# Polysketch attention and a gated FFN in one kernel: batch 0's W from Gram matrices, PSUM copies for VectorE, later key batches in single pieces

## The chip, the cores and the metric

The kernel runs on one core of a Trainium2 chip. The metric is device microseconds of one execution. Kernels are compared on one chip with their runs side by side. Names: TensorE (PE; PEld is its weight load), VectorE (DVE), ScalarE (ACT), GpSimd (POOL), SyncE (SP). SBUF is the working memory, PSUM the memory that matmuls write.

## The reference, cut to what matters

Inputs: q, k, v of 4 batches, 4 heads, 1088 positions, 32 columns; S1, S2 of 8 x 32; three FFN weights (128 x 1536, 128 x 1536, 1536 x 128). All are fp32.

```
phi(x)[.., (i, j)] = a[.., i] * b[.., j]     with a = S1 x, b = S2 x     (r = 8, so 64 features)
kv  = sum over s of phi(k)[s, f] * v[s, d]
z   = sum over s of phi(k)[s, f]
num = phi(q) kv;  den = phi(q) z + 1e-6;  attn = num / den
x   = attn, heads side by side: 4352 rows of 128
out = (relu(x @ w_gate) * (x @ w_val)) @ w_out
```

z as an 8 x 8 matrix Z[i, j] is the sum of a_i b_j over the positions, that is S1 (sum of k k^T) S2^T. The denominator needs no features: phi(q) z = sum over j of b_j(q) (W q)_j, with W[j, d] = sum over i of Z[i, j] S1[i, d]. The kernel calls the 32 x 8 block W of a head "w" and puts it beside S1 and S2 in the stationary operand `wst`, so that one query sketch gives a, b and W q.

## The kernel before, in words

All is laid out by a planner. `Plan.add(engine, cost, function, deps, due, take, give, at)` collects steps, and `Plan.run` (L33) orders them with those costs by the earliest start, among steps within 0.6 us of it by the latest start that `due` allows. Costs, due times (`T0 + PACE * i` for block i of the FFN, L252, L602) and landing times (`land`) only set the order of instructions on each engine; on the chip semaphores hold each instruction until its inputs are there. Where the plan leaves TensorE idle before the first queries are done, matmuls on a zero tile (`warm`, L215, L650) are put in its stream.

PSUM: two double banks `dbl` (slots "V": values, sketches), two single banks `sgl` (slots "G": half a gate each), `o_ps` for the output and `m_ps` (slot "M", one only: sums over keys, transposes of query features, numerators). A step that takes a slot keeps it until a later step gives it back.

Loads: S1 and S2 to `s16`; batch 0's keys in four loads (`load_k`, L138, one for each head) and one for the last 64 rows (`load_kr`), on SP, ScalarE and POOL; the first 8 of 34 query columns of batch 0 (L168), `v32` in two loads. Gate and value weights come on POOL in 8 + 4 blocks of 128 columns, `wo` between. The rest of q, k is issued on SP in order, the rest of v on POOL.

One key batch, class `K` (L255): `t1` transposes 32 x 32 blocks on VectorE, so that head and column lie on the partitions; `sketch` (TensorE, fp32) forms a and b for two pairs of heads; `t2` transposes them back to positions on the partitions (`abk`). `zsum` (L357) sums a b^T over the positions in `m_ps`, `zevac` masks it to heads on VectorE, `w` (L372) multiplies by S1, `wevac` copies it to `wst` on ScalarE. `phi` (L351) forms the features a_i b_j by a broadcast product (`outer`, L245) on POOL, one piece of batch 0 on VectorE; `kv` (L383) sums features times v in `m_ps`; `kvevac` (L392) masks and scales them to `kv_bd` on VectorE. The batch is cut in two pieces (`cuts`). `m_ps` is held from `zsum` to `kvevac`.

The queries go in nine groups, class `Q` (L414): one of 8 columns (256 rows), then eight of 16 (512 rows). `t1`, `sketch` (with `wst`), `t2`, then `bwm`, `red`, `rec`, `am` for 1/den times a, `phi`, `tr` (transposes of the features on TensorE, L503), `tre` (copy on ScalarE), `num`, and `x`, the copy that makes the FFN's input `xT`.

The FFN runs in 51 blocks: `gate` (two halves of 512 columns in two G slots, L553), `relu` on ScalarE, `val` (a V slot), `prod` on VectorE (L565), `outp` (eight matmuls, L570), and at a group's end `oevac` and `store`.

## Time and profile before

| | |
|---|---|
| median of 3 runs | 118.71 us (118.59 to 119.12) |
| the profiled execution | 119.1 us |
| its span | 117.3 us, 3396 instructions |
| DVE busy | 90.3 us, of it products of the FFN (L567) 61.6 |
| ACT busy | 75.6 us, of it relu (L563) 56.2 |
| POOL busy | 51.9 us, of it features of keys 17.8, of queries 17.2 |
| matmuls on zeros (L217) | 190, 14.4 us |
| moved by DMA | 9.49 MB, nearly all before 33 us |

How to read it: times are from the start of the span. Matmuls overlap in the pipeline, so that a row's length for TensorE is longer than the step to the next row; a run of matmuls is read by the distance of its starts. fp32 matmuls are two instructions each. "L" is a line of the kernel. "idle before <- X" names what ended an engine's idle time.

### The profile page before, as it was taken

How to read it: one execution, taken by the hardware profiler on the slowest of the kernel's cores; microseconds unless marked ns; L12 is line 12 of the kernel's file. 1: busy time of each engine (PE TensorE's matmuls, PEld its weight loads, DVE VectorE, ACT ScalarE, POOL GpSimd, SP SyncE). 2: the span in 40 equal slices, each digit the busy share in tenths (PEclk: the TensorE clock that was granted, in tenths of full speed). 3: DMA queues.
4: the chain of work that ended last, by engine and by line, in shares of the span. 5: the costliest groups of instructions: out<-in, count | busy, mean ns of one | idle time of the engine just before them, and what ended most of it. 6: DMA issues, size and time to landing. Idle time of an engine off the chain costs nothing. (4 is left out here: it accounts for less than half of the span.)

```text
span 117.3 us, 3396 instructions
## 1 busy us (share of the span) xinstructions
PE 109.1 (93%) x1381; PEld 72.2 (62%) x1381; DVE 90.3 (77%) x145; ACT 75.6 (64%) x137; POOL 51.9 (44%) x73
## 2 busy tenths in 40 slices
PE   6989999999999999999899999998999999999930
PEld 6968889776665556566555556674566555655620
DVE  4067498687999899669988986799699589678830
ACT  0413003867857996548779874587797897988720
POOL 5708999796360178813401886153107018000000
PEclk9999999999999999999999999999999999999995
DMA  2999999999930030002000300030002003003003
GB/s 75 225 285 261 221 205 219 258 201 228 219 72 0 0 89 8 0 6 67 22 0 6 92 0 6 0 89 0 6 21 69 3 0 92 3 0 95 0 0 89
DMA packets 10908, 9.49 MB, mean 81 GB/s; under 512 B 4420, under 2 KB 9156, under 8 KB 10892
## 3 DMA queue, kind: packets, MB, share of 16 engines
q1 hardware_dynamic: 5364, 6.30, 21.6%
q0 software_dynamic: 4576, 2.05, 13.6%
q10 hardware_dynamic: 952, 0.92, 3.1%
q8 instruction: 10, 0.16, 0.6%
q14 instruction: 6, 0.05, 0.2%
HBM read 9.05 MB, written 2.23 MB: 96 GB/s over the span
## 5 line engine op out<-in xcount | busy, mean ns | idle before, releaser
L567 DVE TENSOR_TENSOR ht<-g_sb,d_ps 128x1024 f16<-128x1024 f16 x51 | 61.6, 1215 | 13.8 <-ACT g_sb L563 9.6
L563 ACT ACTIVATE g_sb<-g_ps 128x512 f16<-128x512 f32 x102 | 56.2, 597 | 16.2 <-PE g_ps L550 15.0
L576 PEld LDWEIGHTS <-ht 128*128 128x128 f16 x408 | 26.7, 113 | 11.3 <-DVE ht L567 3.0
L550 PE MATMUL g_ps<-xT,wg 128*128 128x512 f16 (+1 forms) x108 | 33.2, 368 | 0.2
L576 PE MATMUL o_ps<-wo,ht 128*128 128x128 f16 x408 | 31.2, 220 | 0.8 <-DVE ht L567 0.7
L550 PE MATMUL d_ps<-xT,wv 128*128 128x512 f16 (+1 forms) x108 | 30.3, 367 | 0.0
L246 POOL TENSOR_TENSOR kp<-abk 128x640 f16<-128x640 f32 (+1 forms) x15 | 17.8, 1213 | 5.5 <-DVE abk L347 5.5
L246 POOL TENSOR_TENSOR qp<-an,abq 128x512 f16<-128x512 f32 (+1 forms) x17 | 17.2, 1032 | 0.6
L217 PE MATMUL o_ps<-zero 128*128 128x128 f16 x190 | 14.4, 240 | 1.1 <-DVE mask L201 1.1
L550 PEld LDWEIGHTS <-wv 128*128 128x128 f16 x108 | 9.9, 99 | 7.9 <-issue 1.7
L482 POOL TENSOR_TENSOR bw<-abq 128x128 f32<-128x128 f32 x8 | 3.7, 457 | 24.8 <-DVE abq L472 24.8
L510 ACT COPY pt<-m_ps 128x1024 f16<-128x1024 f16 (+1 forms) x9 | 8.7, 965 | 8.3 <-PE m_ps L506 8.2
L217 PEld LDWEIGHTS <-zero 128*128 128x128 f16 x190 | 12.8, 109 | 2.0 <-DVE mask L201 1.1
L550 PEld LDWEIGHTS <-wg 128*128 128x128 f16 x108 | 8.7, 98 | 5.0 <-issue 1.8
L494 POOL TENSOR_TENSOR an<-abq,rd 128x128 f32<-128x128 f32 x8 | 3.3, 408 | 15.1 <-DVE rd L490 9.6
L472 DVE STREAM_TRANSPOSE abq<-d_ps 128x512 f32<-128x512 f32 (+1 forms) x9 | 6.1, 680 | 1.6 <-PE d_ps L465 1.6
L582 ACT ACTIVATE o_sb<-o_ps 128x512 f32<-128x512 f32 (+1 forms) x9 | 5.1, 572 | 2.1 <-PE o_ps L576 2.0
L506 PE MATMUL m_ps<-ident,qp 128*128 128x128 f16 x68 | 5.3, 219 | 0.9 <-DVE kv_bd L393 0.9
L456 DVE STREAM_TRANSPOSE qT<-qA 128x512 f32<-128x512 f32 (+1 forms) x9 | 5.9, 659 | 0.2 <-DMA qA<-in_q_dram 0.2
L465 PE MATMUL d_ps<-qT,wst 64*64 64x256 f32 (+7 forms) x96 | 5.8, 334 | 0.2 <-ACT wst L379 0.2
L506 PEld LDWEIGHTS <-qp 128*128 128x128 f16 x68 | 4.3, 97 | 2.4 <-issue 1.7
L525 ACT CAST xT<-m_ps 128x512 f16<-128x512 f32 (+1 forms) x9 | 5.2, 578 | 0.6 <-PE m_ps L518 0.6
(67 smaller groups left out, 69.9 us busy)
## 6 DMA issues: line engine op xcount, KB each, us to landing
kA<-in_k_dram SPq DMA_DIRECT2D x14, 128.0 KB, 4.5
out_dram<-o_sb SPq DMA_DIRECT2D x28, 64.0 KB, 1.7
qA<-in_q_dram SPq DMA_DIRECT2D x12, 136.0 KB, 7.2
v_sb<-in_v_dram POOLq DMA_DIRECT2D x3, 256.0 KB, 13.5
v<-in_v_dram ACTq DMA_DIRECT2D x1, 512.0 KB, 7.4
qA<-in_q_dram SPq DMA_DIRECT2D x4, 104.0 KB, 5.3
wo<-in_moe_w_out_dram POOLq DMA_DIRECT2D x1, 384.0 KB, 7.3
kA<-in_k_dram ACTq DMA_DIRECT2D x2, 128.0 KB, 5.3
```

Source lines behind the costliest of these rows:

```text
L217: nc.tensor.matmul(o_ps[:, 0], zero, zero, start=True, stop=True)
L246: eng.tensor_tensor(out=dst.rearrange("p x (i j) -> p x i j", i=R), in0=a[:, :, :, None].to_broadcast([128, n, R, R]), in1=b[:, :, None, : ...
L456: nc.vector.transpose(self.qT.rearrange("p n t -> p (n t)"), qA[:, self.n0:self.n0 + self.nn].rearrange("p n d -> p (n d)"))
L465: nc.tensor.matmul(d[64 * c:64 * c + 64, hp, 32 * lo:32 * hi], wst[r, b].rearrange("p a f -> p (a f)"), self.qT[r].rearrange("p (n c) t -> ...
L472: nc.vector.transpose(self.ab.rearrange("p n a f -> p a n f"), ps(f"q{self.g}")[:, :, 0:32 * self.m].rearrange("p a (n t) -> p a n t", t=32))
L506: nc.tensor.transpose(t[:, 128 * i:128 * i + 128], self.qp[:, i].rearrange("p a f -> p (a f)"), ident)
L510: nc.scalar.copy(out=self.pt.rearrange("f n s -> f (n s)"), in_=m_ps.bitcast(FP16)[:, 0:128 * self.m])
L525: nc.scalar.copy(out=xT[:, 32 * self.n0:32 * (self.n0 + self.nn)].rearrange("p (a t s) -> p a t s", a=4, s=ns), in_=m_ps[:, 0:32 * self.nn ...
L550: nc.tensor.matmul(d[:, (y - lo) * W:(y - lo + 1) * W], w[:, js[y]], xT[:, xs], start=True, stop=True)
L563: nc.scalar.activation(out=g_t[i][:, z], in_=ps1(f"g{i}{z}"), func=ACTF.Relu)
L567: nc.vector.tensor_tensor(out=h_t[i].rearrange("p (a c) -> p a c", a=2), in0=g_t.pop(i), in1=ps(f"v{i}"), op=ALU.mult)
L576: nc.tensor.matmul(o_ps[:, s], ht[:, y * W + s:(y + 1) * W:ns], wo[:, j], start=(j == 0 and s == 0), stop=j == NJ - 1, skip_group_check=True)
```

## The change

The keys of batch 0 are loaded with positions on the partitions, as v is (`k_tok`), in one load of 512 KB on SP and one small one on ScalarE; the small first query load becomes four. A class `K0` takes batch 0. For the three later batches the two pieces become one, `zsum` writes four tiles of 32 rows in a G slot in place of two of 64 rows in `m_ps`, `w` is one matmul in place of two, and `kv_bd` is written by ScalarE in two halves. Where VectorE forms features (batch 0 and the first query group), ScalarE first copies b to a G slot, and VectorE reads it there.

Loads and set-up:

```diff
+    load_v(nc.sync, k_tok, 0, k)
     nc.scalar.dma_start(out=s16[0:R], in_=S1[:, None, :].to_broadcast([R, 4, D]))
-    nc.sync.dma_start(out=s16[R:2 * R], in_=S2[:, None, :].to_broadcast([R, 4, D]))
-    load_kr(nc.gpsimd, 0)
+    nc.scalar.dma_start(out=s16[R:2 * R], in_=S2[:, None, :].to_broadcast([R, 4, D]))
+    load_vr(nc.scalar, k_tok, 0, k)
     for h in range(H):
-        load_k((nc.sync, nc.scalar)[h % 2], 0, h)
-    nc.sync.dma_start(out=qA[:, 0:8, :],
...
+        load_q(nc.sync, 0, h, 0, 8)
     load_v(nc.scalar, v32, 0)
     load_vr(nc.sync, v32, 0)
...
-    warm(48)
+    warm(12)
     nc.tensor.transpose(st_ps, s16x, id32)
+    p_ps = sgl[1][:, 0:128]
+    nc.tensor.matmul(p_ps, s16x[0:R], s16x[0:R], start=True, stop=True)
...
+    st = sb("st", [128, 2 * R])
+    nc.scalar.copy(out=st, in_=st_ps)
+    for hf in range(2):
+        nc.vector.tensor_tensor(out=sk[:, hf, :, hf, :],
...
+    Pbd = sb("Pbd", [128, H, D])
+    nc.vector.tensor_tensor(out=Pbd, in0=p_ps.rearrange("p (h d) -> p h d", h=H),
+                            in1=mask4[:, :, None].to_broadcast([128, H, D]), op=ALU.mult)
...
+    warm(24)
...
-    T0 = 11.5
-    PACE = 1.5
+    T0 = 13.0
+    PACE = 1.4
```

The class for batch 0 (its plan, then the steps on the chip):

```diff
+            ta = add("DVE", 0.66, lambda: self.t1(0, 4), at=land)
+            gram = add("PE", 1.1, self.gram, take=("G", n + "g"), at=land + 0.1, lat=0.2)
...
+            gb = add("DVE", 0.3, self.gevac, [gram])
+            w1 = add("PE", 0.25, self.w1, [gb], lat=0.2)
+            e1 = add("ACT", 0.2, self.w1evac, [w1])
+            w2 = add("PE", 0.25, self.w2, [e1], lat=0.2)
+            self.wst = add("DVE", 0.2, self.wevac, [w2], give=(n + "g",))
+            cast = add("ACT", 1.15, lambda: nc.scalar.copy(out=v_sb[0], in_=v32), at=lvland)
...
+            ca = add("ACT", 0.22, lambda: self.bcopy(0), [ta2], take=("G", n + "b"), lat=0.2)
+            cb = add("ACT", 0.22, lambda: self.bcopy(1), [tb2], take=("G", n + "b"), lat=0.2)
+            pa = add("POOL", 1.06, lambda: self.phi(0, 1, "POOL"), [ta2])
+            pb = add("POOL", 1.06, lambda: self.phi(1, 1, "POOL"), [tb2])
+            da = add("DVE", 0.7, lambda: self.phi(0, 0, "DVE"), [ca])
+            db = add("DVE", 0.7, lambda: self.phi(1, 0, "DVE"), [cb], give=(n + "b",))
+            pr = add("POOL", 0.6, lambda: self.phi(2, 0, "POOL"), [tb2])
+            va = add("PE", 0.25, lambda: self.kv(0), [pa, da, cast], take=("M", n + "m"), lat=0.2)
+            vb = add("PE", 0.3, lambda: self.kv(1), [pb, db, pr, va], lat=0.2)
...
+        def gram(self):
+            d = ps1("k0g")
+            for c in range(NQ):
+                for h in range(H):
+                    nc.tensor.matmul(d[32 * h:32 * h + 32, 0:D], k_tok[:, h, c], k_tok[:, h, c],
+                                     start=c == 0, stop=c == NQ - 1)
...
+        def w1(self):
+            nc.tensor.matmul(ps1("k0g")[:, 64:64 + R], self.gbd.rearrange("p h d -> p (h d)"),
+                             st[:, R:2 * R], start=True, stop=True)
...
+        def w2(self):
+            nc.tensor.matmul(ps1("k0g")[:, 96:96 + R], Pbd.rearrange("p h d -> p (h d)"), self.m1,
+                             start=True, stop=True)
...
+        def sketch(self, x, hf):
+            nc.tensor.matmul(ps("k0")[:, x, 0:256], sk[:, hf].rearrange("p a b f -> p (a b f)"),
+                             self.kT[:, 4 * x + hf:4 * x + 4:2].rearrange("p c h t -> p c (h t)"),
+                             start=hf == 0, stop=hf == 1)
...
+        def bcopy(self, x):
+            nc.scalar.copy(
+                out=ps1("k0b")[:, 64 * x:64 * x + 64].rearrange("p (x j) -> p x j", j=R),
+                in_=self.ab[:, 2 * x:2 * x + 2, :, 0, R:2 * R].rearrange("p c h j -> p (c h) j"))
```

Here P is S1^T S1 (`Pbd`), so that W = P times Gram times S2^T, head by head. The later batches:

```diff
-        def __init__(self, b, land, cuts, engs):
+        def __init__(self, b, land, cuts):
...
+            ab = P.add("PE", 0.75, self.sketch, t1, take=("V", n), lat=0.2)
+            t2 = P.add("DVE", 0.8, self.t2, [ab], give=(n,))
+            z = P.add("PE", 0.65, self.zsum, [t2], take=("G", n + "z"), lat=0.2)
+            zm = P.add("DVE", 0.2, self.zevac, [z])
+            w = P.add("PE", 0.3, self.w, [zm], lat=0.2)
+            self.wst = P.add("ACT", 0.25, self.wevac, [w], give=(n + "z",))
...
+            kv = [P.add("PE", 0.6, self.kv, ph, take=("M", n + "m"), lat=0.2)]
+            kvx = P.add("ACT", 0.25, lambda: kvevac(b, 0), kv)
+            self.kvx = P.add("ACT", 0.25, lambda: kvevac(b, 1), [kvx], give=(n + "m",))
...
+        def zsum(self):
+            d = ps1(f"k{self.b}z")
+            for x in range(NQ):
+                for hp in range(2):
+                    a = self.ab[:, x, hp]
+                    r = 64 * (x % 2) + 32 * hp
+                    nc.tensor.matmul(
+                        d[r:r + 32, 0:2 * R].rearrange("f (h j) -> f h j", h=2),
+                        a.rearrange("p h f -> p (h f)"), a[:, :, R:2 * R],
+                        start=x < 2, stop=x > NQ - 3, skip_group_check=True)
...
+    def kvevac(b, g):
+        nc.scalar.mul(out=kv_bd[b][:, :, D * g:D * g + D],
+                      in_=m_ps[:, 0:128].rearrange("f (h g d) -> f h g d", h=2, g=2)[:, :, g],
+                      mul=maskkv[:, g, 0:1])
```

And the first query group's product on VectorE, with the landing times and the clocks at which the plan begins:

```diff
             if g == 0:
-                ph = [P.add("DVE", 0.62, lambda: self.phi(0, 3, "DVE"), [d4]),
+                bc = P.add("ACT", 0.22, self.bcopy, [t2], take=("G", n + "b"), lat=0.2)
+                ph = [P.add("DVE", 0.52, lambda: self.phi(0, 3, "DVE"), [d4, bc], give=(n + "b",)),
...
-    kk = [K(0, [5.4, 5.4, 5.4, 5.4, 8.5, 5.4], [0, 4, 9], [("DVE", "POOL"), ("POOL", "POOL")])]
-    qland = [7.0, 16.0, 20.0, 24.0]
+    kk = [K0(4.9, 8.0)]
+    qland = [6.5, 16.0, 20.0, 24.0]
...
-        kk.append(K(b, [[0, 14.0, 18.0, 22.0][b]] * 2, [0, 5, 9], [("POOL", "POOL")] * 2))
+        kk.append(K(b, [[0, 14.0, 18.0, 22.0][b]] * 2, [0, 5, 9]))
...
-    order = P.run({"PE": 5.3, "DVE": 5.2, "ACT": 5.2, "POOL": 5.2, "SP": 4.5})
-    pe = 5.3
+    order = P.run({"PE": 4.9, "DVE": 4.8, "ACT": 5.0, "POOL": 5.2, "SP": 4.5})
+    pe = 4.9
```

In the changed program TensorE's stream from the keys of batch 0 to the first gate reads: Gram, half of the sketch, the first W matmul, the other half, the second W matmul, the rest of the sketch, 9 fillers, first query sketch, `kv` first half, 33 fillers, `kv` second half, 19 fillers, second query sketch, transposes of the first queries, 17 fillers, numerator, 14 fillers, gate. On VectorE the transpose of the second query group's columns stands ahead of the first group's product, and on ScalarE the cast of v stands between the two copies of b.

## The prediction

> **What bounds the kernel now.** I read the page, then the timeline of the first 24 us, the chain of waits, and the tables of waits. In the page, the busy line and the chain's first line:
>
> ```profile
> PE 109.1 (93%) x1381; PEld 72.2 (62%) x1381; DVE 90.3 (77%) x145; ACT 75.6 (64%) x137; POOL 51.9 (44%) x73
> ...
> PE 27%; DVE 4%; ACT 3%; issue 1%; ACTq 0%
> ```
>
> TensorE is the engine with the least left (93%), and of the chain that ended last 27% of the span is TensorE against 4% VectorE and 3% ScalarE. That chain reaches back only to 72 us; what lies before is read from the timeline. Its columns are start, length, engine, line, and, last, the instructions merged.
>
> ```profile
> 1.06 4.93 PE L217 MATMUL o_ps<-zero 128*128 128x128 f16 x48 [1.06 <-DVE mask L201]
> ...
> 6.40 1.07 PE L217 MATMUL o_ps<-zero 128*128 128x128 f16 x16
> ...
> 7.25 1.31 DVE L316 STREAM_TRANSPOSE kT<-kA 128x512 f32<-128x512 f32 x2 [0.38 <-DMA kA<-in_k_dram]
> ...
> 9.74 1.15 ACT L304 CAST v_sb<-v 128x1152 f16<-128x1152 f32 x1 [3.03 <-DMA v<-in_v_dram]
> ...
> 10.37 2.98 POOL L246 TENSOR_TENSOR kp<-abk 128x640 f16<-128x640 f32 x2 [0.19 <-DVE abk L347]
> 10.54 1.66 DVE L246 TENSOR_TENSOR kp<-abk 128x512 f16<-128x512 f32 x1
> ...
> 12.47 0.71 DVE L456 STREAM_TRANSPOSE qT<-qA 128x512 f32<-128x512 f32 x1 [0.17 <-DMA qA<-in_q_dram]
> ...
> 13.14 0.57 PE L374 MATMUL m_ps<-zm,S1bd 128*128 128x16 f32 x4
> ...
> 14.23 0.45 PE L465 MATMUL d_ps<-qT,wst 64*64 64x128 f32 x8 [0.16 <-ACT wst L379]
> ...
> 17.62 0.39 PE L506 MATMUL m_ps<-ident,qp 128*128 128x128 f16 x4
> ...
> 19.91 0.60 PE L550 MATMUL g_ps<-xT,wg 128*128 128x256 f16 x4
> ```
>
> This shows two stages. Up to 19.91 us TensorE runs mostly matmuls on zeros (L217), and the first gate matmul (L550) waits for a chain: keys landed and transposed (7.25), products (10.37 and 10.54), W (13.14), the first query sketch (14.23), the transposes of the first query features (17.62). From there 2.3 us lead to the first gate. From 19.91 to 113.2 us TensorE is close to gapless: 51 blocks of gate, value and output matmuls cost 0.43 + 0.43 + 0.45 = 1.31 us each in the chain, 67 of 93 us, and key and query work fills most of the rest. The chain shows what else there is where a key batch ends:
>
> ```profile
> 77.69 0.23 PE g_ps L550
> 77.92 0.02 issue
> 77.95 0.61 ACT g_sb L563
> 78.55 0.02 issue
> 78.58 1.22 DVE ht L567
> 79.80 0.21 DVE kv_bd L393
> 80.01 0.04 issue
> 80.05 0.61 PE m_ps L506 x8
> ```
>
> TensorE's transposes (L506, at 80.05) wait for kv_bd (L393), which stands on VectorE behind a product of 1.22 us (L567). The table of waits prices that at 0.9 us over three batches:
>
> ```profile
> PE m_ps L506 <- DVE kv_bd L393: 0.9, 3, 0.3
> ```
>
> Last, SP's own queue in the first 20 us: a load stands still until v, 512 KB, has landed. The program's loads on SP and ScalarE take eight semaphores in turn, and each waits for the last user of its own.
>
> ```profile
> SPq L139 <- DMA v<-in_v_dram: 1.8, 1, 1.8
> ```
>
> So the time is the start (19.9 us) plus TensorE's work (93.3) plus the tail (4.1). The tail is the same in both orders.
>
> **The change, part by part. The start.** (1) *Keys of batch 0.* Now four loads of 128 KB on two queues; the second on ScalarE's queue lands 5.3 us after its issue at 1.85, so VectorE starts at 7.25, while SP's second (1.65) landed after 3.3, at 5.0. New: all 512 KB first on SP's queue, v behind only S and the 64 last rows on ScalarE's. Bounds: 5.0 (as SP's half now) and 7.2 (as now); I take 5.9, nearer the queue it is moved to. SP's four small q loads come behind, POOL loses one issue of 0.86.
> (2) *Set-up.* Twelve more memsets on VectorE: eight at 0.35/4, two at 0.06, one of 128x256 (0.27), one of 64x128 (0.17): 1.3 us, so they end at 4.5 instead of 3.2; then five masked products instead of two, 0.2 to 0.3 each, to about 5.7. Hidden by the wait for keys, with almost no margin: keys at 5.0 would cost 0.7. S is no limit: its two loads of 4 KB fit in what was moved between 1.0 and 2.3 us (17 GB/s, 22 KB); the second is now issued 0.6 later, so its transposes run near 3.2, with 24 fillers behind.
> (3) *Gram.* 36 fp32 matmuls; the trace shows two instructions per fp32 matmul (L374: x4 for two), so 72. Bounds: 16 instructions of L327 with 64x96 took 0.40 with 0.255 for one, 10 ns each; L361's 18 took 0.77 with 0.22 for one, 32 ns each. 0.7 to 2.3 us; I take 1.4. Sketch of batch 0: eight instructions of L465 with 64x256 took 0.66 on four tiles, so about 0.23 for a pass of 256 columns; two matmuls of full height are four passes, 0.9, twice, and 0.25 for the rest. With the two small W matmuls (0.2 each) TensorE needs 3.9 us from the keys on.
> (4) *W.* Five small steps replace t2, z and W: masked Gram, matmul, copy, matmul, masked copy. W is ready near 9.7 instead of 14.2, since it no longer waits for VectorE's product and for the 38 zero matmuls ahead of L374.
> (5) *b in PSUM.* VectorE's product of 512 took 1.66 beside POOL's (2.98 for two); the one of 384 (16.25, POOL only issuing a DMA) took 0.56, so 512 alone would be about 0.69. New: four of 256 at about 0.42, and two ScalarE copies (0.2 by L379). No less VectorE time, but POOL is not held: 4 x 0.65 + 2 x 0.44 = 3.5 for 4.05. The second copy stands behind the cast of v on ScalarE (1.15), so v's landing enters this path: 9.74 now, with 256 KB of keys ahead. New: 8.0 (those 256 KB at the 279 GB/s of 5 to 10 us, and half the queue's share) to 10.0 (issued 0.3 later); I take 9.0. Then cast to 10.15, copy, product to 11.2. POOL ends near 12.9, with the issue of wo (1.08) now between its products; so kv_bd stands near 14.
> (6) *The queue.* In SP's new order the third of the four wide q loads (columns 8 to 33) reuses v's semaphore, and the fourth and the keys of batch 1 stand behind it. Now only the second key load of batch 1 waits so (the 1.8 above). So they are issued at 9.05 to 9.9 and land 3.9 to 5.3 us later (shortest and median of the q loads): 14.4 against 12.47 now. That transpose (0.71) stands on VectorE ahead of the first queries' product, and the second query sketch on TensorE ahead of the transposes: 14.4 + 0.7 + 0.65 = 15.75 for the transposes, against 17.62.
> (7) From the transposes to the first gate nothing changes: 2.3 us. First gate at 18.1. TensorE's own string from the keys ends sooner: 3.9, 92 fillers at 0.055 (the row at 6.40: 1.07 less 0.24 for one, over 15), and 2.7 for two query sketches, kv, transposes and numerator make 11.7, so 17.6. Gain 1.8; bounds: 3.0 (keys at 5.0, v at 8.0) and 0 (v at 10.0, 5.3 more).
> (8) *POOL's queue.* The last third of wv is issued at 14.93 now, lands 8.2 later at 23.1, and is read at 23.5. New: issued near 14, read at 21.7; with the same 8.2 that is 0.5 late. But wo ahead of it is issued near 10.1 instead of 13.29, so I take 0 and keep 0.5 for the range.
>
> One row speaks against this part. The first 48 zero matmuls took 0.10 each (4.93 less 0.24, over 47), those at 6.40 0.055, though the page's clock row reads 9 in all these slices. The new kernel has 12, a gap, then 24. If half pace lasted through Gram and the first sketch, that is 1.4 + 0.9 = 2.3 more on TensorE's string, of which the wait for q hides 0.5: the gain would be 0. I take no loss, since fillers run from 1.0 on, and keep it as a rival. The Trainium skill (TensorE: Matmul & The Clock Gate, Part 1) has the clock halved until TensorE was busy through a window of about 3.4 us; counted from the gap's end near 3.2 that is an estimated 6.6, half of Gram at half pace, and a gain of 1.6 where the row alone lets me say 1.8.
>
> **The steady part,** three later batches. The W matmul is one, not two: two instructions fewer, 0.113 each (L374: 0.60 for four, 0.26 for one): -0.7. z: 36 instructions of 32-wide tiles for 18 of 64: at 10 to 32 ns, 0.36 to 1.15 for 0.58 a batch; I take 0.02 each, between the tile's own width and its full height, 0.7: +0.4 (-0.6 to +1.7). The Trainium skill (TensorEngine Tiling, Instruction Overhead) gives a matmul about 60 cycles however few its columns, and warns against tiling a dimension already small; at that page's rule, some 25 ns, z alone would be +1.0. Sketch and transposed copy in one piece: one start-up of 0.2 less a batch, -0.3 (0 to -0.6). kv_bd goes to ScalarE in two pieces (0.2 each for 0.28), behind a relu (0.60) instead of a product (1.22): of the 0.9 I take -0.4 (0 to -0.9). m_ps is no longer held from z to kv_bd (25.45 to 33.87 for batch 1), so query transposes can go earlier: -0.3 (0 to -1.0). z now holds one of the two gate buffers: a half gate must wait for a relu of 0.60; the order puts outputs of 0.45 between, so 0.1 a batch: +0.3 (0 to +1.5). New pacing constants only reorder work. Sum -1.0 (-3.8 to +2.5).
>
> **Sum.** The profiled execution took 119.1, span 117.3, so 1.8 lies around it; its span would go to 117.3 - 1.8 - 1.0 = 114.5, that is 116.3. The median of the runs is 118.71, 0.4 lower; taken off that: 115.9.
>
> **The rivals.** *The queue eats the start:* v lands no earlier and the wide q loads land at 15.5 or later; the first gate stays near 19.6. For: the 1.8 wait above and the slow landings; against: v has 256 KB less ahead. 118.7 - 0.3 - 1.0 = 117.4. *Half pace:* no gain at the start, 118.7 - 1.0 = 117.7. For: the 0.10 row; against: it must last 2.3 us past the keys, and TensorE has worked since 1.0 but for the gap. *Slower:* z in the gate buffer. From its matmuls to the copy of W, 2.3 us now (70.71 to 73.0), only one gate buffer is left; if each of four half gates then leaves TensorE idle for 0.38 (relu 0.60 less its own matmul 0.22), a batch loses 1.5, three 4.5, against 1.8 at the start and 1.3 of the steady part without this term: 118.7 - 3.1 + 4.5 = 120.1. It decides from 1.0 us a batch. For: half gates wait so in the chain now; against: outputs stand between. *It does not do what it says:* W was not what the first gate waited for: kv_bd is done at 17.0 now, the first queries' product at 17.3, and if these come no sooner the start gains nothing; with the steady part at the middle of its bounds (-0.6), 118.1.
>
> **How the numbers follow.** Forecast 0.63 (own range 114.0 to 117.3: the start between 1.0 and 2.7, the steady part within 1 of its value), queue 0.13, half pace 0.10, slower 0.08, nothing 0.06. Predicted 115.9. The range takes in the two rivals that eat the start and, below, half of the steady part's better bound: 113.8 to 118.0. A measurement tells 0.5%, 0.6 us, from no change: below 118.1 lie the forecast and most of the first two rivals, 0.83; within, 0.07; above 119.3 the slow rival and the upper tail of the forecast, 0.10.
>
> **What would show it.** The key transpose starting near 5.9; W's masked copy near 9.7; the first gate near 18.1, with the second query transpose waiting for q's DMA just before; the wait of the transposes for kv_bd gone from VectorE; z's 36 instructions near 0.9 us; no relu waits of TensorE around z. Wrong if the first gate stays past 19.5, or if the stretch from first gate to last output is not shorter than 93.3.

## The result: 0.6% faster, and where the gain went

Side by side on one chip, the kernel before took 119.16 us (median of 20 runs) and the changed one 118.56 us; the ratio is 0.9941, 95% interval 0.9915 to 0.9968. The forecast was 115.9 with a range of 113.8 to 118.0: the sign was right, the size was not. Ratios count only undisturbed runs, those within 1.5% of the fastest of their kernel; where that leaves out a whole group of a kernel's runs, its single times are given too.

The page of the changed kernel, busy line and the chain of work that ended last:

```profile
PE 105.0 (90%) x1337; PEld 71.1 (61%) x1337; DVE 90.6 (78%) x157; ACT 78.3 (67%) x149; POOL 50.6 (43%) x76
...
PE 54%; DMA 13%; DVE 11%; ACT 10%; SPq 4%; issue 3%; ACTq 1%; DVEq 0%
```

TensorE is busy for 4 us less than before, which is what the 62 fewer matmuls on zeros make up (14.4 us of busy time before, 10.2 now). But the chain, which reached back only to 72 us before, now goes back to the first load, with 13% of the span in transfers and 4% in SP's queue. So this chain can be read for the start; its columns are start, length and what:

```profile
1.46 0.30 ACTq L166
...
2.52 8.40 DMA v<-in_v_dram
...
10.93 0.31 SPq L154
...
12.44 0.54 SPq L140
...
15.14 0.42 SPq L154
...
16.54 6.79 DMA qA<-in_q_dram
...
23.45 0.06 DVE qT L560
...
24.09 1.18 DVE ht L678
...
27.32 0.55 PE o_ps L687 x8
```

v lands at 10.92. SP's third wide q load (L154) stands until then, behind it the keys of batch 1 (first issued at 12.44; before at 7.43), behind these batch 1's queries (15.14; before 11.75). The last of those lands at 23.3, and VectorE, which meets its transpose (qT) first, starts the FFN's product (ht) only at 24.09. TensorE's and VectorE's waits for it, with SP's own:

```profile
PE m_ps L232 <- DMA s<-in_S_dram: 2.8, 1, 2.8
PE d_ps L661 <- DVE ht L678: 1.1, 1, 1.1
...
DVE qT L560 <- DMA qA<-in_q_dram: 1.7, 1, 1.7
...
SPq L154 <- DMA v<-in_v_dram: 4.0, 1, 4.0
```

Beside that chain runs a second one, on TensorE, which sets the first gate. The timeline, in the columns of the first section (PE and one line of DVE):

```profile
5.37 0.25 PE L232 MATMUL m_ps<-id,s 16*128 16x16 f32 x1 [2.84 <-DMA s<-in_S_dram]
...
6.60 2.74 PE L227 MATMUL o_ps<-zero 128*128 128x128 f16 x24
9.27 1.19 PE L331 MATMUL g_ps<-k_tok 128*32 128x32 f32 x72
10.39 1.60 PE L357 MATMUL d_ps<-kT,sk 128*128 128x256 f32 x4
...
19.04 0.40 PE L617 MATMUL m_ps<-ident,qp 128*128 128x128 f16 x4
...
21.33 0.60 PE L661 MATMUL g_ps<-xT,wg 128*128 128x256 f16 x4
```

S's second load, issued at 1.46 behind the 512 KB of keys, lands at 5.3. TensorE stands for 2.84 us, then runs 24 zero matmuls at 0.107 us each, and Gram starts at 9.27. ("Half pace" is this distance of 0.107 us between the starts of two zero matmuls, "full pace" is 0.056; "the clock rose" names the moment at which one became the other.) The transposes of the first query features (L617) come at 19.04, before at 17.62.

| from the trace | before | changed |
|---|---|---|
| first gate matmul | 19.91 | 21.33 |
| last matmul of the first output block starts | 24.8 | 27.6 |
| last output matmul starts | 112.98 | 112.63 |
| from the second row to the third | 88.14 | 84.98 |

The expectations below call the second row "the eighth output block"; it is the eighth output matmul, the last of the first block. The start lost 2.8 us, the rest gained 3.16, and the span fell by 0.4 (117.3 to 116.9). The two parts are taken in turn.

### The profile page after: what moved, and what is told of

It reads as the page before. It is cut to its first block, busy times and chain, and to the rows that moved or that the text cites. A ratio compares the mean times of both kernels' runs of the same rounds, so it can differ in the third digit from the quotient of the medians.

```text
span 116.9 us, 3336 instructions
## 1 busy us (share of the span) xinstructions
PE 105.0 (90%) x1337; PEld 71.1 (61%) x1337; DVE 90.6 (78%) x157; ACT 78.3 (67%) x149; POOL 50.6 (43%) x76
## 4 chain that ended last, share of the span: by engine, by line
PE 54%; DMA 13%; DVE 11%; ACT 10%; SPq 4%; issue 3%; ACTq 1%; DVEq 0%
PE g_ps L661 16%; PE o_ps L687 15%; PE d_ps L661 13%; DVE ht L678 8%; ACT g_sb L674 8%; DMA v<-in_v_dram 7%; DMA qA<-in_q_dram 6%; PE d_ps L569 4%; SPq L154 2%; PE m_ps L617 2%; PE m_ps L629 2%; SPq L140 2%; PE m_ps L495 1%; ACT xT L636 1%; PE d_ps L441 1%
## 5 line engine op out<-in xcount | busy, mean ns | idle before, releaser
L674 ACT ACTIVATE g_sb<-g_ps 128x512 f16<-128x512 f32 x102 | 57.7, 601 | 14.2 <-PE g_ps L661 12.4
L661 PE MATMUL g_ps<-xT,wg 128*128 128x512 f16 (+1 forms) x108 | 35.4, 367 | 1.4 <-ACT g_sb L674 0.5
L687 PEld LDWEIGHTS <-ht 128*128 128x128 f16 x408 | 28.0, 112 | 10.9 <-DVE ht L678 1.0
L687 PE MATMUL o_ps<-wo,ht 128*128 128x128 f16 x408 | 31.0, 219 | 0.9 <-DVE ht L678 0.9
L586 POOL TENSOR_TENSOR bw<-abq 128x128 f32<-128x128 f32 x8 | 3.6, 456 | 27.6 <-DVE abq L576 27.5
L268 POOL TENSOR_TENSOR kp<-abk 128x640 f16<-128x640 f32 (+1 forms) x12 | 13.8, 1176 | 2.8 <-DVE abk L458 2.8
L661 PEld LDWEIGHTS <-wg 128*128 128x128 f16 x108 | 10.0, 100 | 5.6 <-issue 2.6
L227 PE MATMUL o_ps<-zero 128*128 128x128 f16 x128 | 10.2, 245 | 1.1 <-DVE mask L207 1.1
L227 PEld LDWEIGHTS <-zero 128*128 128x128 f16 x128 | 9.0, 112 | 1.4 <-DVE mask L207 1.1
L268 POOL TENSOR_TENSOR kp<-ab 128x256 f16<-128x256 f32 (+1 forms) x6 | 3.1, 551 | 8.1 <-DVE ab L367 8.1
L617 PE MATMUL m_ps<-ident,qp 128*128 128x128 f16 x68 | 5.5, 220 | 0.1
## 6 DMA issues: line engine op xcount, KB each, us to landing
v_sb<-in_v_dram POOLq DMA_DIRECT2D x3, 256.0 KB, 10.2
```

The source lines that it names most:

```text
L227: nc.tensor.matmul(o_ps[:, 0], zero, zero, start=True, stop=True)
L268: eng.tensor_tensor(out=dst.rearrange("p x (i j) -> p x i j", i=R), in0=a[:, :, :, None].to_broadcast([128, n, R, R]), in1=b[:, :, None, : ...
L617: nc.tensor.transpose(t[:, 128 * i:128 * i + 128], self.qp[:, i].rearrange("p a f -> p (a f)"), ident)
L661: nc.tensor.matmul(d[:, (y - lo) * W:(y - lo + 1) * W], w[:, js[y]], xT[:, xs], start=True, stop=True)
L674: nc.scalar.activation(out=g_t[i][:, z], in_=ps1(f"g{i}{z}"), func=ACTF.Relu)
L687: nc.tensor.matmul(o_ps[:, s], ht[:, y * W + s:(y + 1) * W:ns], wo[:, j], start=(j == 0 and s == 0), stop=j == NJ - 1, skip_group_check=True)
```

## Experiments on the start

All are compared with the kernel before; "first block" is the start of the last matmul of the first output block in the profiled execution. The stretch from there to the last output matmul was 84.98 or 84.99 in every run of this section but e13_warm40, where it was 85.85.

| run | change against the changed kernel | median us | ratio, 95% | first gate | first block |
|---|---|---|---|---|---|
| (changed) | | 118.56 | 0.994 (0.992-0.997) | 21.33 | 27.6 |
| e1_sfirst | S ahead of the keys | 115.72 | 0.968 (0.962-0.975) | 18.78 | 23.9 |
| e2_q | batch 0's q in two loads | 117.44 | 0.986 (0.982-0.990) | 20.61 | 26.2 |
| e3_sq | both | 114.91 | 0.963 (0.959-0.968) | 18.29 | 23.5 |
| e10_nofill | 24 zero matmuls taken out | 118.40 | 0.991 (0.986-0.995) | 21.95 | 27.5 |
| e13_warm40 | zero matmuls 40 + 0 for 12 + 24 | 120.39 | 1.000 (0.993-1.007) | 19.75 | 28.4 |
| e17_qwarm | two q loads, 48 + 0 | 118.37 | 0.988 (0.981-0.996) | 21.75 | 26.9 |
| e19_s2sp | S2 on SP's queue behind the keys | 118.74 | 0.992 (0.988-0.996) | 21.77 | 27.7 |

**S ahead of the keys, e1_sfirst.**

```
+    (ScalarE: S1)
+    nc.sync.dma_start(out=s16[R:2 * R], in_=S2...)
     load_v(nc.sync, k_tok, 0, k)
-    nc.scalar.dma_start(out=s16[R:2 * R], in_=S2...)
```

> The changed kernel with both loads of S issued ahead of the 512 KB of keys (S1 on ScalarE's queue, S2 first on SP's). Theory (S late behind the keys, then 24 zero matmuls at half pace): the transposes of S start near 3 us instead of 5.37, the Gram matmuls near 6.5 instead of 9.27, the first gate near 19.7 instead of 21.33, and the time falls by 1.0 to 1.5 us against the changed kernel (about 117.3). Rival (v's landing and the queue behind it hold the first gate anyway): Gram starts sooner, but the first gate stays within 0.4 us of 21.33 and the time within 0.4 us.

Two loads of 4 KB in another order bring 3.1 us (0.9941 - 0.9684, times 119.2), more than expected (the six runs are 114.9, 115.0, 115.4, 116.1, 117.3 and 119.4). TensorE's timeline in this run:

```profile
2.47 0.27 PE L232 MATMUL m_ps<-id,s 16*128 16x16 f32 x1
...
3.71 2.74 PE L227 MATMUL o_ps<-zero 128*128 128x128 f16 x24
6.38 0.89 PE L331 MATMUL g_ps<-k_tok 128*32 128x32 f32 x72
...
18.78 0.60 PE L661 MATMUL g_ps<-xT,wg 128*128 128x256 f16 x4
```

The rival fell: the first gate moved by 2.55 us. But not S alone had moved. SP's queue hardly waited for v any more (0.7 and 0.9 us), and batch 1's keys were issued from 7.97 on instead of 12.44. The transfers between 4.5 and 6.5 us show why; first the changed kernel, then e1, total and ScalarE's queue (q10, with v) and POOL's (q0, with the gate and value weights):

```profile
DMA packets 446, 0.39 MB, mean 196 GB/s; under 512 B 118, under 2 KB 402, under 8 KB 446
...
q10 hardware_dynamic: 324, 0.25, 51.3%
q0 software_dynamic: 44, 0.09, 27.3%
```

```profile
DMA packets 956, 0.70 MB, mean 350 GB/s; under 512 B 322, under 2 KB 938, under 8 KB 956
...
q10 hardware_dynamic: 780, 0.55, 84.9%
...
q0 software_dynamic: 18, 0.04, 11.2%
```

With S first, ScalarE's queue moves 0.55 MB in these 2 us, which is nearly all of v and the last keys; in the changed kernel 0.25, and v drags on beside the weights until 10.9. So one line of order changed S, the clock and v together, and this run does not part them.

**The queue alone, e2_q.**

```
-    for h in range(H):
-        load_q(nc.sync, 0, h, 0, 8)
+    (one load of columns 0 to 8, all heads; one of columns 8 to 34)
```

> The changed kernel with batch 0's queries in two loads instead of eight (first 8 columns, then the other 26, all heads in each), so that no load on SP reuses v's semaphore. Theory (SP's queue standing 4.0 us behind v makes batch 1's q late, and that stalls the first FFN blocks): the 4.0 us wait of SP's queue is gone, batch 1's keys are issued before 9 us instead of 12.44, the transpose of q at 23.45 no longer waits 1.7 us for its load, the TensorE stall of 1.29 us at 24.0 is gone, and the time falls by 1.0 to 1.5 us (about 117.3). Rival (the stall comes from VectorE's own backlog): the loads come sooner, the stall of over 1 us stays, and the time stays within 0.4 us.

The time fell by 1.0 us (0.9941 - 0.9856), and the 1.1 us wait of TensorE fell to 0.4. But SP's queue still stands behind v; it now does so at the last rows of batch 1's keys (L144), and longer:

```profile
SPq L144 <- DMA v<-in_v_dram: 6.8, 1, 6.8
```

The edit moved the wait and did not take it away: batch 1's other keys are now ahead of it, issued from 3.48 on instead of 12.44, but its queries are issued at 13.70, only 1.4 us sooner. The chain goes another way:

```profile
2.54 10.43 DMA v<-in_v_dram
13.00 1.16 ACT v_sb L309
...
14.20 0.39 PE m_ps L393 x8
```

Loads issued sooner share the engines with v, which now lands at 12.97; the kv sums wait for its cast. The queue behind v was one bound, and v itself is the next one. (The clock rose at 9.1 in this profile and W was ready at 12.9, but TensorE then waited for the cast, so that neither set the first gate.)

**Both, e3_sq:** the two diffs above together.

> Both edits: S ahead of the keys and batch 0's queries in two loads. If the two losses lie one behind the other, as the theory has it, the gains add: 2.0 to 3.0 us below the changed kernel (about 116), the first gate near 19.7 and the eighth output block below 26 instead of 27.6. Rival (both hide behind the same limit, v or VectorE): no more than the better of the two alone.

114.91 us, ratio 0.963: 3.7 us below the changed kernel, less than the sum of both (4.1). The first gate is at 18.29, where the forecast had 18.1; this is partly chance, since W was 1.2 us later than forecast (10.9 for 9.7) and the way from W to the gate 1.1 us shorter (7.3 for 8.4).

**Without the 24 zero matmuls, e10_nofill** (`warm(24)` becomes `warm(0)`).

> The changed kernel without the 24 zero matmuls that stand between S's small matmuls and Gram; S is as late as before. Theory (S's lateness and the zero matmuls are two halves of one loss): Gram starts near 6.7 instead of 9.27, still at half pace, the first gate near 19.5 instead of 21.3, time 1.2 to 2.5 us under the changed kernel. Rival (only S's lateness matters, the zero matmuls raise the clock and pay for themselves): Gram starts sooner but runs longer at half pace, and the time is within 0.5 us of the changed kernel.

The rival: Gram started 2 us sooner and nothing came of it. Its chain of waits:

```profile
1.46 3.91 DMA s<-in_S_dram
...
7.26 1.19 PE g_ps L331 x72
8.45 2.02 PE d_ps L357 x4
...
11.00 2.08 PE d_ps L357 x4
...
27.14 0.55 PE o_ps L687 x8
```

The sketch's two halves took 2.0 and 2.1 us where 1.13 is their time in e1: without zero matmuls the half pace lasted to about 15.6. The zero matmuls cost what they bring.

**TensorE kept busy while S is awaited, e13_warm40** (`warm(12)`, `warm(24)` become `warm(40)`, `warm(0)`).

> The changed kernel with 40 zero matmuls ahead of S's small matmuls and none behind them, instead of 12 and 24: S lands as late as before (its matmuls at about 5.4), only four zero matmuls more, but TensorE works through until S is there. Theory A (the loss was the clock: the gap of 3 us while S was awaited put the rise to full clock off to about 11): the clock rises between 3.9 and 6.5, S's matmuls take half of their 1.25 us, Gram starts near 6.3 and takes 0.6 to 0.9, the first gate comes at 18.0 to 19.0 and the time falls by 2.0 to 3.0 us under the changed kernel, about 116. Theory B (the loss was S's landing itself): Gram starts near 6.5, but no more than half of that gain comes, the time is above 117.3.

The six runs are 118.5, 119.0, 120.2, 120.6, 120.6 and 121.0. All lie where theory B had them, but not for B's reason, and A was not put to the test: in the profiled execution (120.2) the clock rose only at about 10. Gram came 2.0 and the first gate 1.6 us sooner all the same, and the first output block later than ever (28.4). The chain goes by the queue behind v, with TensorE off the path:

```profile
2.52 8.82 DMA v<-in_v_dram
...
13.72 6.28 DMA kA<-in_k_dram
...
24.40 1.18 DVE ht L678
```

The clock also fell back. The granted clock, full in the changed kernel at that time, is 0.82, 0.50 and 0.82 here from 26 to 28, 28 to 30 and 30 to 32 us; the first eight output matmuls take 1.03 us for 0.62 (L687), and what follows up to 30.7 is slowed as well, which is the likely reason for the longer stretch of 85.85. The middle row, with its times, its length, the busy time of PE, PEld, DVE, ACT and POOL, the granted clock, and the DMA engines' share and GB/s:

```profile
28.00:30.00 2.00, 2.00 (x15) 1.69 (x13) 0.26 (x1) 0.95 (x2) 2.00 (x3) 0.50 1.17 226
```

**The same with two q loads, e17_qwarm** (`warm(48)`, `warm(0)`).

> The run with batch 0's queries in two loads (117.44 us, eighth output block at 26.2; SP's queue no longer behind v, S still late) with 48 zero matmuls ahead of S's small matmuls and none behind, for 12 and 24. Theory A (what S's lateness costs is the clock, held at half pace by the gap in TensorE's work): full clock between 3.9 and 6.5, Gram near 6.8 at 0.6 to 0.9 us, first gate 18.0 to 19.2, eighth block 23.4 to 24.5, time 115.0 to 116.2. Theory B (S's landing itself): Gram starts at 6.5 to 7.0 too, but the time stays above 116.8. If the clock again rises only near 10 in the profiled execution, the time is 116.5 to 117.5 and the runs scatter by over 1 us.

Full pace came at about 7.1 and Gram at 7.89 in 0.83 us, W at 11.8, and still the time was above 116.8 in all six runs (117.0, 118.0, 118.0, 118.8, 120.3, 121.4), as theory B had it, but for a reason neither had named: TensorE then waited 2.6 us for v's cast. SP's queue stood 7.8 us for v at L144, as in e2.

```profile
2.55 11.57 DMA v<-in_v_dram
14.14 1.16 ACT v_sb L309
...
15.34 0.39 PE m_ps L393 x8
```

**S2 out of v's way, S still late, e19_s2sp.**

```
-    nc.scalar.dma_start(out=s16[R:2 * R], in_=S2...)
+    nc.sync.dma_start(out=s16[R:2 * R], in_=S2...)
```

> The changed kernel with one line moved: S2's load goes on SP's queue behind the 512 KB of keys, instead of on ScalarE's queue ahead of the last keys and v. S stays late (it lands behind the keys, about 5 us), all zero matmuls and the query loads stay. Theory (the blocked S2 at the head of ScalarE's queue holds back v, which then shares the engines with the weights on POOL's queue; v late is what makes SP's queue stand): v's cast starts before 11 us instead of 12.65, SP's wait for v falls from 4.0 to 2 us or less, batch 1's first key load is issued before 10 us instead of 12.44, and the eighth output block comes at 25.5 to 26.5 instead of 27.6 (what is left, against 23.9 with S ahead, is S and the clock): time 116.7 to 117.7. Rival A (v was all of it): 116.3 or less. Rival B (only S's landing and the clock count): within 0.5 us of the changed kernel.

The time did not change (ratio 0.992), but the run does not speak for rival B: v landed at 10.76, 0.16 sooner, SP still waited 4.3 us for it, and the chain is the changed kernel's, piece for piece. So S2 in ScalarE's queue is not what holds v back.

What follows for the start: three things were late side by side, v and the queue behind it, S, and with S the clock. Runs that ease one or two of them leave the first output block at 26 to 28 us, held by what is left (e2 and e17 by v, e13 by the queue, e10 by S and the half pace); only S's place ahead of the keys eases all. That is shown; how the 3.1 us divide among the three is not, since no run cures the queue alone or S alone. e1 and e19 issue the same loads and differ on SP's queue only in whether S2 stands ahead of the keys or behind them, so it is this order that decides how fast v moves. Why it does, and why the weights' packets then start a microsecond later (their issue is at 2.60 in both), is open.

## Experiments on what comes next

| run | on top of e3_sq | median us | ratio, 95% | first gate | first block |
|---|---|---|---|---|---|
| e6_warm | zero matmuls 30 + 10 for 12 + 24 | 114.88 | 0.968 (0.966-0.971) | 16.97 | 23.6 |
| e14_less | and a quarter fewer later | 115.51 | 0.973 (0.971-0.976) | 16.22 | 24.2 |
| e15_ql18 | 30 + 10, one transpose moved | 115.18 | 0.957 (0.949-0.964) | 17.29 | 22.4 |
| e15_ql20 | 30 + 10, more steps moved | 114.88 | 0.957 (0.950-0.964) | 18.91 | 24.3 |
| e18_warm44 | e15_ql18 with 44 + 4 | 114.89 | 0.963 (0.955-0.971) | 18.32 | 24.1 |

```
e6:   -  warm(12) ... warm(24)             +  warm(30) ... warm(10)
e14:  -  warm(int((...) * 1.1 / 0.056))    +  warm(int((...) * 0.8 / 0.056))
e15:  -  qland = [6.5, 16.0, 20.0, 24.0]
      +  qland = [6.5, 18.5, 22.0, 26.0]   (e15_ql18)
      +  qland = [6.5, 20.0, 22.0, 26.0]   (e15_ql20)
e18:  -  warm(30) ... warm(10)             +  warm(44) ... warm(4)
```

> The version with S ahead and queries in two loads (114.91 us), with 30 zero matmuls ahead of S's small matmuls and 10 behind them, instead of 12 and 24: the same work but two, in an order that leaves TensorE no thin stretch at 2.5 to 3.7 us. Theory (the clock rises only after an unbroken stretch of work: at 5.44 and 3.95 us in two kernels with 48 zero matmuls in a row, at 6.53 and 8.1 with 12, S and 24): the pitch of the zero matmuls falls to 0.056 us between 3.9 and 5.5, Gram takes 0.6 to 0.9 instead of 1.19, the first sketch 0.9 instead of 1.27, and the first gate comes 0.5 to 1.2 us before 18.29. Rival (the moment is set by something else, or the chain behind the sketch hides it): the first gate within 0.3 us of 18.29.

The clock rose at about 4.3, Gram took 0.83, W was ready at 9.6, the first gate came 1.3 us sooner, all nearly as expected, and the time stayed. VectorE's timeline has the reason: it comes to batch 1's queries before they have landed, and the product stands behind them.

```profile
19.38 0.71 DVE L561 STREAM_TRANSPOSE qT<-qA 128x512 f32<-128x512 f32 x1 [1.99 <-DMA qA<-in_q_dram]
20.01 1.18 DVE L679 TENSOR_TENSOR ht<-g_sb,d_ps 128x1024 f16<-128x1024 f16 x1
```

> The same with the zero matmuls between the steps of the start cut by about a quarter (factor 0.8 instead of 1.1 in the fill rule). Up to the first gate TensorE is without a gap in the version at 114.91 us, so that zero matmuls end up to 0.36 us after the operand behind them is ready. Theory: another 0.5 to 0.9 us off the first gate, about 113.5 us. Rival (the gaps halve the clock again, as in the version without the 24): the first gate no sooner, the time the same or longer.

The first gate came at 16.22, and the time rose by 0.6 us: there was no more to win there (the wait for ht remained, 1.1 us), and the transposes of the second group now waited 0.6 us for POOL. The rival was also right in part: in this profile the granted clock is 0.85, 0.50 and 0.80 from 20 to 22, 22 to 24 and 24 to 26 us, so the clock fell back behind these two waits. How many of the other runs share that is not known.

> The version with 30 and 10 zero matmuls (114.88 us, first gate 16.97) with one instruction moved: VectorE's transpose of the third query group, which stood at the head of its queue for 2.0 us until batch 1's q had landed at 19.4, comes behind the first FFN product and the transpose of the key sketch. Theory (that wait gives back the 1.3 us by which the first gate came sooner): the wait of TensorE for ht of 1.3 us is gone, the eighth output block comes at 22.3 to 22.8 instead of 23.6, time 113.8 to 114.2. Rival (the transfers of the start, with the DMA engines at 9 tenths until 31 us, limit these blocks anyway): another wait for a DMA takes its place, the time stays above 114.5.

In the profiled execution (113.5 us) the wait is gone and the first output block comes at 22.4. The other runs show it only in part: 113.5 and 113.6, then 115.2, 115.2, 115.3 and 115.7.

> The same with the landing of the later q's put at 20, 22 and 26 in the plan (for 16, 20 and 24), which moves the key sketch of batch 2 and some transposes of later groups behind a block of the FFN too. Expected: the start as in the run with one instruction moved; the rest of the order is new, so the stretch from the eighth output block to the last may go either way from 84.98 by up to 1 us.

Again two groups, 113.3 and 113.4 against 114.8 to 115.4. This profile is one of 115.2 us: the same instructions at the start, but the sketch's matmuls fall from 0.43 us each to 0.22 only at 9.0, where full pace was there by 5.2 in the profile above. With that Gram moved from 6.04 to 6.81 and the first gate by 1.6 us. Gram in e15_ql18, then here:

```profile
6.04 0.83 PE L332 MATMUL g_ps<-k_tok 128*32 128x32 f32 x72
```

```profile
6.81 1.19 PE L332 MATMUL g_ps<-k_tok 128*32 128x32 f32 x72
```

The 1.7 us between the two executions lie in the start. That the other runs of each group differ in the same way is likely and not shown: each group has one profile, of two kernels.

> The version with S ahead, two query loads, 30 and 10 zero matmuls and the one moved transpose (runs at 113.5 or 115.2; in the profiled execution at 113.5 the clock was full from about 5, in the same start profiled at 115.2 from about 9), with 44 and 4 zero matmuls: an unbroken stretch of about 4 us instead of 3.2 ahead of S's small matmuls. If the length of that stretch decides whether the clock rises before Gram, most runs lie at 113.3 to 114.2. If the moment is a matter of phase that 44 do not reach either, the two groups of runs stay.

Not settled by length: the six runs are 114.4, 114.5, 114.6, 115.2, 116.1 and 116.3. In the profiled one the clock rose at 5.5, and the 44 zero matmuls at half pace had themselves put Gram off to 7.08. The lowest ratio, 0.957, is that of the two versions with moved transposes: 113.3 to 113.6 us in their better runs, about 115 in the others, against 118.56 and 119.16. By the medians all versions with 30 or 44 zero matmuls and unchanged fillers lie between 114.9 and 115.2.

## Experiments on the steady part

```
e4:   batch 0, its loads and T0 = 11.5, PACE = 1.5 as in the kernel before;
      class K of the changed kernel for batches 1 to 3
e5:   the kernel before, with  T0 = 13.0, PACE = 1.4
e12:  e4 with  T0 = 13.0, PACE = 1.4
```

> The kernel before with only the later batches changed: batch 0 as it was (four key loads, z and W as before, start constants 11.5 and 1.5), batches 1 to 3 in single pieces, z by 32-wide tiles in the gate slot, kv_bd on ScalarE. Theory (the 3.1 us that the stretch from the eighth output block to the last lost come from these batch edits): first gate near 19.9 as before, time 2 to 3 us under the kernel before (about 116.3). Rival (the 3.1 us come from the other pacing constants, or are only backlog that a late start makes up): within 0.8 us of the kernel before.

The kernel before with only the later batches changed: 117.40 us, ratio 0.981 (0.976 to 0.987), stretch 86.08; the six runs are 116.5, 116.8, 116.9, 117.9, 118.5 and 119.5. The batch edits alone bring 2.2 us; 2.06 of the 3.16 us of the stretch are theirs. (In this profile the first gate came 1.13 us sooner, at 18.78, as the first transpose of keys started at 6.12 instead of 7.25: the clock rose at 4.0 and not at 5.4, which brought the masked products of S 0.7 us sooner, and the keys had landed by then.)

> The kernel before with nothing but the two pacing constants of the change (first block 13.0 for 11.5, pace 1.4 for 1.5). Theory (the constants only reorder work; the gain of the steady part comes from the batch edits): time within 0.6 us of the kernel before, and the stretch from the eighth output block to the last within 0.6 us of its 88.14. Rival (the order is worth about a third of the 3.1 us: the changed kernel's stretch is 84.98, with the old constants and the new batches it was 86.08): the stretch falls by 0.8 to 1.5 us.

The constants 13.0 and 1.4 in the kernel before: 121.55 us, ratio 1.017 (1.013 to 1.022), stretch 88.82. Neither expectation: alone they cost 2 us, with three waits of TensorE for xT of 1.7 us in sum. "They only reorder work" was wrong as a price.

> The version with only the later batches changed (117.4 us, stretch from the eighth output block to the last 86.08), with the changed kernel's constants 13.0 and 1.4. Theory (with the new batches the constants are worth the missing 1.1 us, though in the kernel before they cost 2): stretch 84.7 to 85.4, time near 116.3. Rival (the 1.1 comes from batch 0's other order, which frees slots sooner): stretch 85.8 or above.

Stretch 85.38 as the theory had it, time 116.56, ratio 0.983 (0.979 to 0.986): the ratio is that of e4_steady, since the first gate was later by 0.9 us (34 zero matmuls became 48 ahead of the transposes). With the new batches the constants are worth 0.7 us of the stretch; the last 0.4 is left to batch 0's order, which no run isolates.

The next two start from e3_sq (114.91) and take one batch edit back; the rest of the order follows from the planner.

```
e8:  -  kvx = P.add("ACT", 0.25, kvevac(b, 0)); self.kvx = P.add("ACT", 0.25, kvevac(b, 1))
     +  self.kvx = P.add("DVE", 0.28, self.kvevac, kv, give=(n + "m",))
e9:  -  z = P.add("PE", 0.65, self.zsum, [t2], take=("G", n + "z"), lat=0.2)
     +  z = P.add("PE", 0.65, self.zsum, [t2], take=("M", n + "m"), lat=0.2)
```

> The version with S ahead and queries in two loads (114.91 us, stretch from the eighth output block to the last 84.98), with kv_bd of batches 1 to 3 back on VectorE in one instruction. If kv_bd on ScalarE is what the steady part gained most by, the stretch rises by 1.0 us or more (86 or above) and the waits of TensorE's transposes for kv_bd return. If it was worth the 0.4 us of the prediction or less: 84.8 to 85.5.

115.94 us, ratio 0.971 (0.967 to 0.976) for 0.963: kv_bd on ScalarE is worth about 1.0 us. Where it is won is not shown. The stretch was 86.21, but in an execution of 117.4 us, above the others, in which the granted clock fell back (0.50 from 24 to 26 us); and the transposes' wait for kv_bd, which was to return, is not among TensorE's waits there.

> The same version (114.91 us, stretch 84.98) with z and W of batches 1 to 3 back in m_ps, which is then held from z to kv_bd, and no longer in a gate buffer. If the freed m_ps is the main gain, the stretch rises by 1.0 us or more. If it is worth the 0.3 us of the prediction, and z in the gate buffer costs about as much, the stretch stays within 0.5 us. Slower rival of the prediction (z in the gate buffer costs over 1 us a batch): the stretch falls by 1 us or more.

116.46 us, ratio 0.977 (0.973 to 0.981): the freed m_ps, less what z costs in the gate buffer, is worth about 1.6 us, and the stretch grew by 1.4 (86.36). TensorE then waits at the numerators and the gate:

```profile
PE g_ps L663 <- ACT xT L638: 0.7, 1, 0.7
PE m_ps L631 <- ACT kv_bd L280: 0.6, 1, 0.6
```

In the changed kernel neither stands among TensorE's waits. The forecast's slower rival, z in the gate buffer, would have made this run faster; it fell.

**b in PSUM, e11_bsbuf** (e3_sq without the copies; VectorE reads b from SBUF).

```
-  ca = add("ACT", 0.22, lambda: self.bcopy(0), ...); cb = add("ACT", 0.22, lambda: self.bcopy(1), ...)
-  bc = P.add("ACT", 0.22, self.bcopy, ...)
   (outer on VectorE takes b from ab, as on POOL)
```

> The version at 114.91 us without the copies of b to PSUM: VectorE's products of batch 0 and of the first queries read b from SBUF. Theory (VectorE and POOL hinder each other when both read SBUF: 1.66 us for 512 columns before, 0.75 for two of 256 with b in PSUM): the two of 256 take 1.2 to 1.7 us instead of 0.75 where POOL's run beside them, POOL's own 1.21 to 1.5, and the first gate comes 0.5 to 1.0 us later, time plus 0.4 to 1.0. Rival (other steps hide it): the products are slower, the first gate within 0.3 us.

115.55 us, ratio 0.975 (0.972 to 0.978) for 0.963: the copies are worth 0.6 us by the medians, 1.4 by the ratios, and 0.8 us at the first gate. VectorE beside POOL in this run:

```profile
9.27 1.19 DVE L269 TENSOR_TENSOR kp<-ab 128x256 f16<-128x256 f32 x2
...
12.02 1.65 DVE L581 TENSOR_TENSOR bw<-abq 128x64 f32<-128x64 f32 x1
13.59 0.97 DVE L269 TENSOR_TENSOR kp<-ab 128x256 f16<-128x256 f32 x2
```

With b in PSUM the two pairs took 0.75 and 0.74, and the small product of 64 columns 0.59 (it reads SBUF in both runs, and here it started beside POOL's next four products); POOL's pair beside the first took 1.21, here 1.62. The Trainium skill (SBUF — State Buffer, SBUF: two separate sides) has one port pair that VectorE with two SBUF inputs and POOL take in turn for whole instructions. These rows agree that the two hinder each other while both read SBUF, but not with whole instructions in turn: both first pairs ended within 1.66 us, where one after the other would make 1.96 (0.75 and 1.21).

## Why the prediction was wrong, step by step

In the forecast's own terms, the first gate was to come 1.8 us sooner and came 1.4 later (21.33 for 18.1, a miss of 3.2), while from the first gate to the last output the time fell by 1.8 for 1.0 (93.3 to 91.5). So the term of the start is what failed, and in it steps (2) and "half pace": S 2.2 us late and 24 zero matmuls at half pace 1.25 are the 3.4 us by which Gram started late (9.27 for 5.9). The queue, step (6), came on top, behind the first gate.

- **(1) Keys.** They landed at 5.0 (0.81 and 4.2 us to landing), the better bound, not at 5.9. It did not matter: VectorE's first transpose started at 6.99, behind five masked products that waited for S.
- **(2) "S is no limit": wrong.** It was argued from the bytes that moved between 1.0 and 2.3 us before. Of the second load it was priced that it was issued 0.6 us later, not that 512 KB were issued ahead of it. It landed at 5.3, and TensorE's transposes came at 5.37 instead of 3.2. Put ahead of the keys, S brought 3.1 us (e1), v and the queue included.
- **(3) Gram and sketch** were sized for full pace: 0.83 and 1.13 us in e6_warm, for 1.4 and 0.9. In the changed kernel they took 1.19 and 1.60.
- **Half pace, "taken as no loss": wrong.** The row against it (0.10 a zero matmul) was the right one. Its price of 2.3 was made of the wrong parts: 1.4 and 0.9 for Gram and the sketch, which lost 0.4 and 0.5 against e6_warm, and nothing for the zero matmuls: 24 at 0.107 for 0.055 are 1.25 us. And half pace lasted 6 us from the gap's end (5.4 to 11.4), where the forecast's estimate had 3.4.
- **(4) W** was stored at 14.0, not 9.7; in e6_warm, with S early and the clock up, at 9.6. The working from the keys to W was right, its two conditions were not met.
- **(5) v and b.** The products with b in PSUM took 0.375 for the 0.42 forecast, and the hindrance by POOL went. v landed at 10.9, outside the bounds of 8.0 to 10.0: the upper one was today's landing plus 0.3 us of later issue, with nothing for the company it would have. This term heads the chain.
- **(6) The queue: priced at the wrong consumer.** It was seen that the fourth q load and batch 1's keys stand behind v, but only batch 0's own transpose was priced; that one did not even wait (17.38): the fourth load, issued at 11.29, landed 2.8 us later, near the forecast's 14.4. The cost sat further back: batch 1's queries issued 3.4 us later than before, 1.7 us of VectorE, 1.1 of TensorE. From the first gate to the first output block it took 6.3 us for 4.9 before. Together with v, S and the clock this made 2.8 us lost at the first block where 1.8 were to be won.
- **(7)** From the transposes to the first gate 2.3 us, as said. **(8)** wv cost nothing, as taken.
- **Steady part**: right in sign; -1.0 for -1.8 from the first gate on, or for -3.16 behind the first block. kv_bd was worth 1.0 for 0.4; m_ps and z in the gate buffer together 1.6, where -0.3 and +0.3 had cancelled. A likely reason: the table of waits prices the waits of one order, and a freed slot lets the planner make another. The sign "no relu waits of TensorE around z" did not come true; behind z of batches 2 and 3 the gate waits for a relu:

```profile
PE g_ps L661 <- ACT g_sb L674: 0.5, 2, 0.2
```

z was taken at +0.4, because 36 matmuls replace 18; the groups of z by line, before and then changed, say the reverse:

```profile
L361 PE MATMUL m_ps<-abk 128*64 128x32 f32 x72 | 3.3, 225 | 0.2
```

```profile
L472 PE MATMUL g_ps<-abk 128*32 128x16 f32 x108 | 1.6, 185 | 0.2 <-DVE abk L458 0.2
```

For four batches 3.3 us of busy time, for three 1.6: 0.8 a batch against 0.5. In the trace the 36 on 32-wide tiles start 9 to 11 ns apart on average (7 within each four), the 18 on 64-wide tiles 32 ns apart (7 and 52 by turns). The Trainium skill (TensorEngine Tiling, Instruction Overhead) would have made z dearer; the trace decides against it here.
- **Rivals.** "Half pace" came true as a mechanism. "The queue eats the start" came true in its effect and not by its sign: not the wide q loads of batch 0 were late but batch 1's queries. No case had held both together; the gain of the steady part, unforeseen in size, paid for them. "Slower" fell: the waits for a relu above are 0.5 us and not 4.5, and without z in the gate buffer (e9) the kernel was slower. "Does not do what it says" fell for the first gate: it came 7.34 or 7.35 us after the copy of W ended in eleven profiles, with W at 14.0 (changed) as at 9.6 (e6), along the same string of fillers and small steps on TensorE; fewer fillers made it 6.6 (e14). It holds for the first block, for which the queue's chain counted as well.

## What to carry to other kernels

Write the first loads in the order in which their consumers start, the small ones first: 4 KB behind 512 KB cost 3 us here. Where a change makes a queue stand, follow every load behind it to its last consumer, not only the next one. And when a first milestone moves and the time does not, read what the in-order engines meet next: three times here (e6, e13, e14) a sooner first gate only met the next late transfer.

## What the runs showed of the hardware

- TensorE's start-to-start distance for a zero matmul is 0.107 us at first and 0.056 later, while the page's clock row reads 9 throughout: the trace's list of granted clock begins, with full clock, only at the moment of the fall (5.45 us before, 11.37 changed), and the page counts the time ahead of it as full. With zero matmuls in a row from 1.06 on, the fall came at 3.9 to 5.5 us in eight profiles, but at 7.1 in e17_qwarm and only at 9.0 and 10.2 in e15_ql20 and e13_warm40, where the row had ended at 4.4 and 5.5; with S's small matmuls at 2.5 to 3.9, at 6.3 to 8.6 in five profiles (6.5 in e1, 8.1 in e3); with the gap of 2.5 to 2.9 us, at 9.1 (e2), 11.4 (changed) and 12.2 (e19), and without zero matmuls behind the gap at 15.6 (e10). The same start gave 5.1 and 9.0 in two profiles, 1.6 us at the first gate.
- The moments lie on a grid. In e13 the granted clock changes at 10.23, 27.30 and 30.71 us, steps of 17.07 and 3.41 us, that is five times 3.41 and once. In e8 and e14 too it fell for 3.41 us, behind waits of TensorE of 1.1 to 1.5 us; behind the wait of 1.1 us in the changed kernel it did not. The Trainium skill (TensorE: Matmul & The Clock Gate, Part 1) has a free-running window of 3.4 us that must be busy, so a run-to-run scatter; it puts the rise at about 4 us into steady work, give or take half a microsecond. Here, from the first zero matmul on, it came after 2.8 to 4.4 us in the eight profiles and after 6.0 in e17.
- In the changed kernel as in e1, ScalarE's queue moved 40 packets between 1.5 and 4.0 us, though its loads were issued from 0.81 to 2.52 on. Nearly all other packets of that time were SP's queue's with the keys, and they kept the engines busy for only 60% of it (changed) and 41% (e1); so want of engines alone does not explain why ScalarE's queue stood; the reason is open.
